# Batch 1's X units one loop step sooner, and a reordered opening, in a one-core Fourier mixer with an ELU MLP

## The chip, the cores and the metric

The kernel runs on one core of a Trainium2 chip. The core has a matrix engine (TensorE, PE in the profile, with PEld for its weight loads), a vector engine (VectorE, DVE), an activation engine (ScalarE, ACT), a general engine (GpSimd, POOL) and a queue engine (SyncE, SP) that issues DMAs. POOL issues DMAs too, on a queue of its own. Each engine works through its own instructions in program order; semaphores join them. The metric is the device time of one execution in microseconds (us).

## What is computed

The input x is 8 batches of 3008 tokens by 256 channels, in f32. For every batch a real Fourier transform runs along the tokens, a complex 256 x 256 product with a bias follows, each part is shrunk towards zero by 0.01, and the inverse transform goes back to tokens. The result passes an MLP with 2048 hidden columns and an ELU.

```python
X = np.fft.rfft(x, axis=1)
Yr = Xr @ w_r - Xi @ w_i + b_r
Yi = Xr @ w_i + Xi @ w_r + b_i
Yr = np.sign(Yr) * np.maximum(np.abs(Yr) - lam, 0.0)
y = np.fft.irfft(Y, n=x.shape[1], axis=1)
h = y.reshape(B * S, D) @ w_in
g = np.where(h > 0.0, h, np.exp(np.minimum(h, 0.0)) - 1.0)
out = g @ w_out
```

## The kernel before

**The transform as matmuls.** 3008 = 47 x 64, and the Fourier transform is split into two stages over these factors, as is its inverse. One batch passes these units:

- A (`unit_A`, lines 155 to 216; six per batch): the first stage, on a quarter of an x tile of 1 MB. Its result goes to the tile Z, in the opening by DMA straight from the copied block (`place`, L197), later through DRAM (DA, L216, and `load_Z`, L222).
- X (`unit_X`, L224; eight per batch): the second stage, Z times M2 (L237), copied into XT.
- M (`unit_M`, in the opening `first_M` and `last_M`; six pairs): the complex product with wcat, bias and shrinkage, giving Y. `turn_Y` (L428) turns Y through four DMAs on SP (L423).
- B (`unit_B`, in the opening `split_B`; six per batch): the first inverse stage. Its result goes to DRAM (DB) by a DMA on SP and comes back regrouped as Bs (`load_Bs`, L468).
- Y (`unit_Y`, `split_Y`, in the opening `first_Y`; eight per batch): the second inverse stage, Bs times M4, copied into yT.

**The loop.** Tokens are then taken in blocks of 512, and hidden columns in 8 pairs of 128. One step of the loop (line 1296) is one block and one pair: `front` computes two h tiles (L1098) and their exponential Et on ACT (L1110); `elu` clamps Et on POOL (L1149) or DVE (L1151); in the next step `finish_elu` forms gT on DVE (L1139); two steps later `back` multiplies by w_out (L1170) and stores a finished block from SP (L1191). A batch is 47 steps. While the loop works on batch b, the units of batch b+1, and the A units of batch b+2, are woven into its steps by `plan(b)` (L1200): list f0 of a step is issued ahead of `front`, list f1 behind it. For batch 0 the first step with an X unit of batch 1 is `FILL` (L1060); up to then the steps hold batch 1's A units (steps 0 to 5, with their DMAs to DRAM, `load_Z` in step 5) and the last Y units of batch 0 (`split_Y`, steps 7 to 9), which use a PSUM pool psG that is closed at step FILL. From FILL on, the list `mid` (L1206) is worked off one unit per step. `load_Bs` of batch 1 is issued in the step of B5 and in later steps.

**The opening.** All that is ahead of the loop is written out by hand (lines 612 to 1048), under a manual schedule, so the order of the program text is the order of each engine's queue. In turn:

1. `idle_pe(3)` (L620): filler matmuls on ones, while constants are built and x of batch 0 arrives by POOL's DMAs (`first_x`). An f32 matmul of the filler shows as two instructions.
2. The matrices M1d and M1c of the A units: cleared on ACT (L689), filled on DVE (L754, L761) from the sines r1 (L745, ACT). Z is cleared on ACT (L683).
3. Tables for X (M2) from DVE (`points`, `wraps`, `sizes`, `signs`, L805 to L835) and ACT (`sines`, L838), with a correction of its row 0 on DVE (`slot0`, L850); beside them on DVE the start of M3's tables (L863 to L869).
4. The six A units of batch 0 (L183). Units in `FOUR` sum four x rows per output with M1d (16 matmuls, one placing DMA), the others two with M1c (8 matmuls, two placing DMAs). Units run in two PSUM slots (pre2, two banks each), which ACT empties in order (L150); unit 5 runs in two single banks.
5. A second filler, `idle_pe(4)`, then the eight X units; the weights w_r and w_i come by SP and are cast to wcat on POOL, behind a gate (L911) and among `load_x` of batch 1.
6. The M pairs in the order 3, 4, 5, 0, 1, 2, with B units 3, 4, 5 between. Y is finished in halves: the last step of a pair that went over ACT is held and issued on DVE by `let_go` (L351). Pieces of w_in (`load_w_in` on SP, four) are scaled and cast to w_in_s on DVE or POOL (`scale_w_in`, L950). w_out comes in two halves by POOL (`load_w_out`, L945), each behind a `gate`, a small POOL copy that waits for a given tile (L958).
7. The seam: for B units 0 to 2, the part of Bs that the first Y units need is not sent through DRAM but turned on PE (`turn_B` L536, `turn_back` L559); the rest of it comes by `load_Bs(0, 0, 48)` (L474). Then `first_Y` (L577) and the remaining B units 0 to 2 (`split_B`, L492), whose copies and stores are issued by `store`.

Of the kernel before, what the change touches and what calls it, by code (L numbers as in the profile page):

```python
# [29 lines left out]
def kernel(  # L30
# [122 lines left out]
    FOUR = (0, 1, 2, 4, 5)  # L153

    def unit_A(b, u, alone=False, on_dve=False, apart=False):
# [324 lines left out]
    def split_B(v, ps, on_dve=(False, True), by_half=False):  # L480
# [24 lines left out]
        def store():  # L505
            for s in range(2):
                evac(Bv[:, s], ps[s][:].rearrange("p (q d) -> p q d", d=D), on_dve[s])
# [4 lines left out]
        return (lambda: half(1), store) if by_half else store  # L512
# [4 lines left out]
    def one_bank():  # L517
        return chain.tile([P, 512], F32, name="one", tag="one")
# [35 lines left out]
    def turn_back(dt):  # L554

        for h in range(2):
            ps = one_bank()
# [10 lines left out]
    def first_Y(dt):  # L568
# [4 lines left out]
        for h in range(2):  # L573
            ps = one_bank()
# [41 lines left out]
    def idle_pe(n):  # L616

        ones = busy[:].bitcast(F32)
        for _ in range(n):
            nc.tensor.matmul(  # L620
                ips[-1][:].rearrange("p (a b) -> p a b", a=2), lhsT=ones[:, 0:P],
                rhs=ones.unsqueeze(1).to_broadcast([P, 2, 256]), start=True, stop=True,
# [3 lines left out]
    idle_pe(3)  # L626
# [4 lines left out]
    with tc.tile_pool(name="stagep", bufs=1) as stagep:  # L631
# [61 lines left out]
        clear(M1d[:].rearrange("p q w -> p (q w)"))  # L693

# [51 lines left out]
        clear(M1c[:].rearrange("p q w -> p (q w)"))  # L746
        for h in range(2):
            clear_Z(h)
        c1 = mix(dve, qcol, -2.0, pcol, ALU.mult, ALU.add)
        c0 = col(dve, c1, -1.0, ALU.mult, 1.0, ALU.add)  # L750
        for h, c in enumerate((c0, c1)):
            for q in range(2):
                o = 3 * NS + 16 * h + 8 * q
                dve.tensor_scalar(  # L754
                    M1d[:, :, o : o + 8],
                    r1[:, NS * q : NS * q + NS].rearrange("p (b a) -> p a b", a=4),
                    c[:], None, ALU.mult,
                )
        r1v = r1[:].rearrange("p (q b a) -> p q a b", q=2, a=2)
        for h, c in enumerate((c0, c1)):  # L760
            dve.tensor_scalar(  # L761
                M1c[:, :, N2 + NS * h : N2 + NS * h + NS].rearrange("p a (q b) -> p q a b", q=2),
                r1v, c[:], None, ALU.mult,
            )
# [91 lines left out]
        def fA(u):  # L856
            unit_A(0, u, alone=True, apart=u == 5)
# [5 lines left out]
        dve.tensor_scalar(m3i[:], m3i[:], 63, None, ALU.bitwise_and)  # L863
        k3 = row("k3", [P, NV])
        dve.scalar_tensor_tensor(k3[:], m3i[:], float(N1), k1t[:], ALU.mult, ALU.add)
        dve.tensor_scalar(sg3[:], k3[:], S // 2 + 0.5, -0.5, ALU.is_gt, ALU.add)
        full = [P, NV, N2]
        k3b = k3[:].unsqueeze(2).to_broadcast(full)
        dve.scalar_tensor_tensor(  # L869
            v3[:], n2row.unsqueeze(1).to_broadcast(full), 1.0 / S, k3b, ALU.mult, ALU.mult  # L870
# [502 lines left out]
```

## Time and profile before

| what | value |
|---|---|
| median of the runs | 876.56 us (3 runs, 874.92 to 877.61) |
| the profiled execution | 874.79 us |
| its span in the trace | 873.0 us |
| PE busy | 862.9 us, 99% of the span |
| ACT, DVE, POOL busy | 713.9, 666.2, 587.1 us |
| first X unit of batch 0 on PE | 21.38 us |
| first `front` matmul | 45.71 us |
| first X unit of batch 1 on PE | 68.42 us |

Times in the profile count from the start of the span. A row of the timeline gives start, length, engine, line, operation, what is written from what, shape and count, and in brackets how long the engine was idle before and what ended that. A row of the waits gives engine and line that waited, for whom, total, number and longest. A row of the chain of waits gives start, length and what the end of the execution hung on at that time. SPq and POOLq are DMA issues. A busy PE need not be PE at its peak, since matmul ends are modelled.

### The profile page before, as it was taken

The page shows a single profiled execution, that of the slowest core. Times are in us where ns is not written, and L with a number is a line of the kernel's source. Part 1 is how long each engine was busy: PE and PEld are TensorE (multiplying, and loading weights), DVE is VectorE, ACT ScalarE, POOL GpSimd, SP SyncE. Part 2 cuts the span into 40 slices and gives each one's busy share as a digit, 9 for nine tenths or more (in the row PEclk, how much of TensorE's full clock was granted, in tenths as well). Part 3 has the DMA queues.
Part 4 walks back from the last instruction along what each step waited for, and adds up shares of the span by engine and source line. Part 5 has one row for each costly group of instructions (what it writes and reads, how often), then busy time and mean ns, then how long its engine had stood idle before and what let it go on. Part 6 is the DMA issues. An engine that isn't in the chain of part 4 may idle for free.

```text
span 873.0 us, 18541 instructions
## 1 busy us (share of the span) xinstructions
PE 862.9 (99%) x6768; PEld 675.8 (77%) x6768; DVE 666.2 (76%) x1110; ACT 713.9 (82%) x1251; POOL 587.1 (67%) x859
## 2 busy tenths in 40 slices
PE   9999999999999999999999999999999999999997
PEld 6567677887788877887779787788777878787776
DVE  8888778687776876768866787777777677788775
ACT  7778888888978889798887988879887888876664
POOL 7761640898757986588856888459874697734664
PEclk9999999999999999999999999999999999999999
DMA  8997346542474225743356442653337313250111
GB/s 242 297 279 200 112 113 191 166 143 76 122 242 130 89 73 147 217 147 101 94 169 182 133 110 73 203 160 119 100 89 214 97 38 86 75 144 25 39 36 49
DMA packets 115596, 116.11 MB, mean 133 GB/s; under 512 B 11552, under 2 KB 106016, under 8 KB 112144
## 3 DMA queue, kind: packets, MB, share of 16 engines
q1 hardware_dynamic: 109248, 87.40, 35.5%
q0 software_dynamic: 5968, 27.26, 9.9%
q8 instruction: 53, 0.87, 0.4%
q14 instruction: 39, 0.32, 0.1%
q10 hardware_dynamic: 288, 0.26, 0.1%
HBM read 53.28 MB, written 48.23 MB: 116 GB/s over the span
## 4 chain that ended last, share of the span: by engine, by line
PE 92%; POOL 2%; DMA 2%; DVE 1%; ACT 1%; issue 0%; SPq 0%; DVEq 0%; POOLq 0%
PE ps_o L1170 38%; PE hps L1098 34%; PE mps L329 5%; PE xps L237 3%; PE mps L1098 2%; PE yps L604 2%; PE bps L443 2%; PE aps L191 2%; PE mps L287 1%; PE ips L620 1%; DMA Bs<-DB 1%; PE aps L183 1%; POOL Y L345 1%; DMA DB<-Bz 1%; POOL yb L341 0%
## 5 line engine op out<-in xcount | busy, mean ns | idle before, releaser
L1139 DVE SCALAR_TENSOR_TENSOR gT<-Et,hps 128x512 fp32r<-128x512 f32 x630 | 402.9, 683 | 136.9 <-POOL Et L1149 127.0
L1170 PE MATMUL ps_o<-w_out_r,gT 128*128 128x256 f32 x3008 | 477.3, 301 | 0.0
L1170 PEld LDWEIGHTS ps_o<-w_out_r,gT 128*128 128x128 f32 x3008 | 404.4, 189 | 48.1 <-DVE osb L1182 0.2
L1149 POOL TENSOR_SCALAR Et<-Et 128x512 f32<-128x512 f32 x482 | 288.0, 617 | 209.3 <-ACT Et L1110 207.8
L1098 PE MATMUL hps<-yT,w_in_s 128*128 128x512 bf16 (+7 forms) x1620 | 366.1, 353 | 0.2
L1110 ACT ACTIVATE Et<-hps 128x512 f32<-128x512 f32 x514 | 282.5, 609 | 41.3 <-PE hps L1098 37.5
L1098 PEld LDWEIGHTS <-w_in_s 128*128 128x128 bf16 x1728 | 144.2, 98 | 103.9 <-issue 12.4
L1108 ACT ACTIVATE Et<-hps 128x512 f32<-128x512 f32 x192 | 104.6, 597 | 41.9 <-PE hps L1098 41.5
L1113 ACT ACTIVATE Et<-Et 128x512 f32<-128x512 f32 x192 | 110.4, 631 | 0.0
L345 POOL TENSOR_TENSOR Y<-yb,clip 128x512 bf16<-128x512 f32 x72 | 92.7, 1288 | 6.0
L341 POOL TENSOR_TENSOR yb<-yb,bias_bc 128x256 f32<-128x256 f32 x72 | 53.2, 739 | 11.4 <-DVE yb L336 11.4
L150 ACT CAST XT<-xps 128x768 bf16<-128x768 f32 x57 | 45.9, 805 | 13.7 <-PE xps L237 13.6
L150 ACT CAST yT<-yps 128x752 bf16<-128x752 f32 x56 | 44.1, 788 | 14.5 <-PE yps L604 14.5
L336 DVE TENSOR_TENSOR yb<-mps,yb 128x512 f32<-128x512 f32 x72 | 49.8, 692 | 7.6 <-PE hps L1098 0.5
L1141 DVE SCALAR_TENSOR_TENSOR gT<-hps,Et 128x512 fp32r<-128x512 f32 x78 | 50.2, 686 | 3.3
L150 ACT CAST A<-aps 128x1024 bf16<-128x1024 f32 x41 | 41.7, 1018 | 9.6 <-PE aps L191 4.9
L344 POOL TENSOR_SCALAR clip<-yb 128x512 f32<-128x512 f32 x72 | 44.3, 615 | 6.3
L150 ACT CAST Bz<-bps 128x1024 bf16<-128x1024 f32 x41 | 41.6, 1015 | 5.2 <-PE bps L443 4.9
L335 DVE TENSOR_TENSOR yb<-mps,bias_bc 128x256 f32<-128x256 f32 x72 | 30.5, 424 | 17.4 <-PE mps L329 15.6
L329 PE MATMUL mps<-wcat_s,XT 128*128 128x256 bf16 x288 | 43.2, 273 | 0.0
L1182 DVE COPY osb<-ps_o 128x512 f32<-128x512 f32 x46 | 31.7, 690 | 5.4 <-PE ps_o L1170 3.4
L255 POOL TENSOR_TENSOR XS<-XT 128x512 bf16<-128x512 bf16 x30 | 34.1, 1162 | 2.4 <-ACT XT L150 1.4
(208 smaller groups left out, 666.5 us busy)
## 6 DMA issues: line engine op xcount, KB each, us to landing
xt<-in_x_dram POOLq DMA_DIRECT2D x21, 1024.0 KB, 5.4
out_dram<-osb SPq DMA_DIRECT2D x158, 128.0 KB
Bs<-DB SPq DMA_DIRECT2D x30, 384.0 KB
Yx<-Y SPq DMA_DIRECT2D x168, 64.0 KB
DA<-A SPq DMA_DIRECT2D x19, 512.0 KB
DB<-Bz SPq DMA_DIRECT2D x19, 512.0 KB
Z<-DA SPq DMA_DIRECT2D x21, 384.0 KB
xt<-in_x_dram POOLq DMA_DIRECT2D x6, 512.0 KB, 5.8
```

The source lines that it names most:

```text
L150: nc.scalar.copy(dst, src)
L329: nc.tensor.matmul(out_, lhsT=lhs[:, dt] if lhs is not None else sum_of(dt, ch)[:, oc : oc + P], rhs=w[:, dt, :], start=(dt == 0), stop=(d ...
L341: nc.gpsimd.tensor_tensor(yb[:, D : 2 * D], yb[:, D : 2 * D], bias_bc[:, D : 2 * D], ALU.add)
L345: nc.gpsimd.tensor_tensor(Y_of[b, q][:, i, :], yb[:], clip[:], ALU.subtract)
L1098: nc.tensor.matmul(hps[s][:, c0:c1], lhsT=w_in_s[:, dt, ft * P : ft * P + P], rhs=yT_of[b][:, dt, t0 : t0 + c1 - c0], start=(dt == 0), sto ...
L1108: nc.scalar.activation(Et[:, s], hps[s], AF.Relu, scale=-1.0)
L1110: nc.scalar.activation(Et[:, s], hps[s], AF.Exp)
L1113: nc.scalar.activation(Et[:, s], Et[:, s], AF.Exp, scale=-1.0)
L1139: nc.vector.scalar_tensor_tensor(o, e, -1.0, h, ALU.add, ALU.max)
L1141: nc.vector.scalar_tensor_tensor(o, h, 0.0, e, ALU.max, ALU.add)
L1149: nc.gpsimd.tensor_scalar(e, e, 1.0, 0.0, ALU.min, ALU.max)
L1170: nc.tensor.matmul(po[q][:, i_ % 2, :], lhsT=gT[:, s, i_ * P : i_ * P + P], rhs=w_out_r[:, ft, :], start=(ft == 0 and i_ % 2 == 0), stop=( ...
```

## The change

It has two groups of edits.

*Loop.* `FILL` falls from 10 to 9, so that the list `mid` starts one step sooner and the `split_Y` units of batch 0 go to steps 6 to 8. In `mid`, B5 changes places with A0 and so stays in step 35; A3 goes ahead of the first two Y units, which stay in steps 39 and 40. The scaling of the second half of w_in piece 1 leaves step 1.

*Opening.* Unit A2 works with two x rows per output instead of four, in the two begin banks, each half copied and placed by itself. M1d and M1c are filled on ACT instead of DVE, with M1c cleared ahead of r1 and Z cleared behind the fills. M1 is filled on POOL instead of ACT. Parts of the tables change places: `signs(1)` and the second `sines(1, 1)` sooner, the m3i to v3 group later. Both fillers are half a matmul shorter. `load_w_in` 1 to 3 and the scalings of pieces 0 and 1 are issued sooner. `let_go` is issued once more ahead of `load_Bs`. Both halves of w_out are loaded without gates behind M4, with `load_x(1, 2)` between them, and so behind `load_Bs` in the program. At the seam, `split_B(1)` goes between the halves of `turn_B(2)`, the copies of `split_B(0)` are split (the ACT half ahead of `turn_back`, the DVE half and the store behind it), and the pool chain of four banks becomes chain and chain2 of two.

```diff
-    FOUR = (0, 1, 2, 4, 5)
+    FOUR = (0, 1, 4, 5)
...
-            pair = two_banks(pre1, "mps1") if alone else two_banks(psG, "gps")
+            if alone:
+                pair = two_banks(begin, "begin") if u == 2 else two_banks(pre1, "mps1")
+            else:
+                pair = two_banks(psG, "gps")
...
-            if alone:
+                if alone and u not in FOUR:
+                    place(2 * j, 2 * j + 2)
+            if alone and u in FOUR:
                 place(0, 4)
...
-    idle_pe(3)
+    idle_pe(2)
+    idle_pe(1, 1)
...
         clear(M1d[:].rearrange("p q w -> p (q w)"))
+        clear(M1c[:].rearrange("p q w -> p (q w)"))
...
         nc.scalar.activation(r1[:], v1[:], AF.Sin, bias=0.0, scale=TURN / 4.0)
-        clear(M1c[:].rearrange("p q w -> p (q w)"))
-        for h in range(2):
-            clear_Z(h)
...
-                dve.tensor_scalar(
+                nc.scalar.activation(
                     M1d[:, :, o : o + 8],
                     r1[:, NS * q : NS * q + NS].rearrange("p (b a) -> p a b", a=4),
-                    c[:], None, ALU.mult,
+                    AF.Copy, scale=c[:],
                 )
...
+            for q in range(2):
+                nc.scalar.activation(
...
+        for h in range(2):
+            clear_Z(h)
...
-            unit_A(0, u, alone=True, apart=u == 5)
+            unit_A(0, u, alone=True, apart=u in (2, 5))
...
         sizes(1)
+        signs(1)
+        dve.tensor_scalar(m3i[:], m3i[:], 63, None, ALU.bitwise_and)
...
         slot0()
+        for h, c in enumerate((c0, c1)):
+            pool.tensor_scalar(M1[:, N2 * h : N2 * h + N2], r1[:], c[:], None, ALU.mult)
         sines(1, 0)
+        sines(1, 1)
...
-        load_x(1, 2)
         for q, i in ((3, 0), (3, 1)):
             begin_M(q, i)
-        idle_pe(4)
+        idle_pe(3)
+        idle_pe(1, 1)
...
     load_w_in(0)
+    load_w_in(1)
...
     fB(3)
-    load_w_in(1)
+    load_w_in(2)
     first_M(5, 1, True)
+    for c in range(2):
+        scale_w_in(0, True, c)
     first_M(0, 0, False)
     fB(4)
-    scale_w_in(0, True, 0)
+    for c in range(2):
+        scale_w_in(1, True, c)
     first_M(0, 1, True)
     fB(5)
-    gate(Bz_of[0, 2][:, 7, 0:1])
-    load_w_out(0)
+    let_go()
     load_Bs(0, 0, 16 * NT)
-    load_w_in(2)
+    load_w_in(3)
     first_M(1, 0, False)
-    scale_w_in(0, True, 1)
-    scale_w_in(1, True, 0)
...
-    load_w_in(3)
     M4v = M4[:].rearrange("p (a h) -> p a h", h=2)
...
+    load_w_out(0)
+    load_x(1, 2)
+    load_w_out(1)
     first.close()
...
     turn_B(2, (0,), two_banks(chain, "one"), True)
-    turn_B(2, (1,), two_banks(chain, "one"), True)
-    store_0()
-    rest_1, store_1 = split_B(1, two_banks(lateB, "lateB"), (True, True), True)
+    rest_1, store_1, _ = split_B(1, two_banks(lateB, "lateB"), (True, True), True)
+    turn_B(2, (1,), two_banks(chain2, "one"), True)
+    copy_0(0)
     turn_back(0)
     turn_back(1)
+    store_0((1,))
     rest_1()
-    gate(Y_of[0, 2][:, 1, 0:1])
-    load_w_out(1)
...
-    FILL = 10
+    FILL = 9
...
-            ("B", 2), ("M", 5, 0), ("M", 5, 1), ("B", 3), ("B", 4), ("B", 5), ("A", 0),
-            ("A", 1), ("A", 2), ("n", 0), ("n", 1), ("A", 3), ("A", 4), ("A", 5),
+            ("B", 2), ("M", 5, 0), ("M", 5, 1), ("B", 3), ("B", 4), ("A", 0), ("B", 5),
+            ("A", 1), ("A", 2), ("A", 3), ("n", 0), ("n", 1), ("A", 4), ("A", 5),
...
-                (7, f0, 2), (7, f1, 3), (8, f0, 4), (8, f1, 5), (9, f0, 6), (9, f1, 7)
+                (6, f0, 2), (6, f1, 3), (7, f0, 4), (7, f1, 5), (8, f0, 6), (8, f1, 7)
...
-            f1[1].insert(0, (scale_w_in, (1, True, 1)))
```

More of the change, by code (lines that the diff above doesn't have):

```diff
@@ L510, in store, with one_bank @@
             )
-        return (lambda: half(1), store) if by_half else store
+        return (lambda: half(1), store, copy_out) if by_half else store
     NT = 3
     turned = []
-    def one_bank():
-        return chain.tile([P, 512], F32, name="one", tag="one")
+    def one_bank(dt):
+        return (chain2 if dt else chain).tile([P, 512], F32, name="one", tag="one")
     def turn_B(v, ts=(0, 1), ps=None, on_dve=False):
```

54 lines of the change are left out of this document (26 added, 28 removed).

## The prediction

> **What bounds the kernel now.** I read the page first (busy times), then the TensorE (PE) waits, then the timeline of the first 75 us and of 113 to 145 us, the chain of waits there, and the DMA issues with their landings.
>
> ```profile
> span 873.0 us, 18541 instructions
> PE 862.9 (99%) x6768; PEld 675.8 (77%) x6768; DVE 666.2 (76%) x1110; ACT 713.9 (82%) x1251; POOL 587.1 (67%) x859
> ```
>
> PE is busy for 862.9 of 873.0 us, so a change pays only if it removes PE work, PE filler, or one of PE's waits. The waits of PE over the whole span are short; these are the five that matter here (us in total, times, longest):
>
> ```profile
> PE yps L604 <- DMA Bs<-DB: 0.7, 1, 0.7
> PE one L577 <- DMA Bs<-DB: 0.5, 1, 0.5
> PE lateB L536 <- DVE Y L351: 0.5, 1, 0.5
> PE bps L443 <- DMA Yx<-Y: 0.4, 1, 0.4
> PE lateA L492 <- DVE Y L351: 0.3, 1, 0.3
> ```
>
> They sum to 2.4 us. Three of them (one, lateB, lateA) stand at the seam between the opening and the loop, two (bps, yps) at the border from batch 0 to batch 1. What else can be won is filler and A work ahead of the first X unit, because all that follows shifts with it.
>
> **Opening, up to X.** The timeline (start, length):
>
> ```profile
> 1.45 4.62 PE L620 MATMUL ips<-busy 128*128 128x512 f32 x6 [1.45 <-DVE busy L613]
> 4.13 0.26 ACT L745 ACTIVATE r<-v 128x64 f32<-128x64 f32 x1 [1.07 <-DVE v L744]
> 4.22 1.95 POOL L121 DMA_DIRECT2D xt<-in_x_dram  x3
> 4.46 0.81 DVE L754 TENSOR_SCALAR M1d<-r,c 128x32 fp32r<-128x32 f32 x4
> 4.71 3.70 ACT L683 ACTIVATE Z<-busy 128x2048 f32<-128x2048 bf16 x2
> 5.53 6.29 PE L183 MATMUL aps<-xt,M1d 128*128 128x256 f32 x48
> 8.32 0.98 ACT L150 CAST A<-aps 128x1024 bf16<-128x1024 f32 x1
> 12.93 2.16 PE L183 MATMUL aps<-xt,M1d 128*128 128x256 f32 x16 [0.15 <-ACT A L150]
> 17.02 0.59 ACT L150 CAST A<-mps 128x512 bf16<-128x512 f32 x1 [0.36 <-PE mps L183]
> 17.66 3.70 PE L620 MATMUL ips<-busy 128*128 128x512 f32 x8
> 19.11 0.38 DVE L850 TENSOR_SCALAR M<-M,c 128x24 bf16<-128x24 bf16 x2 [0.34 <-ACT M L838]
> 19.40 1.14 DVE L835 SCALAR_TENSOR_TENSOR a<-a,c,sw 128x384 f32<-128x384 f32 x2
> 19.71 0.58 ACT L904 ACTIVATE M<-r,c 128x64 fp32r<-128x64 f32 x2
> 21.38 0.84 PE L237 MATMUL xps<-M,Z 128*128 128x96 bf16 x16
> ```
>
> The reader sees a chain: A units on PE, the last A copy on ACT until 17.61, filler from 17.66 to 21.36, X at 21.38. The last copy and the filler set the start of X.
>
> *Unit A2 twofold.* It falls from 16 to 8 matmuls. At 6.29/48 = 0.13 us each that is 1.05 us of PE work gone. It also moves to the begin banks, so that A4 no longer waits for A2's copy (the 0.15 in its row). Begin's banks are next used by the two bias matmuls after A5, long after A2's copy. A2 gets one placing DMA more on SP, an issue of some 0.57 us (two take 1.14 in the row of 131.60 below). Its two halves are copied by ACT in about the time of one whole copy and more than 3 us ahead of A5's copy, so SP is free again when A5's own DMA is due, and nothing behind it is late.
>
> *Fills move from DVE to ACT.* DVE loses the M1d fill (0.81) and the M1c fill (two instructions, so less than another 0.81). ACT gains eight copies of 128x32, four for each tile. No row shows one; the nearest is L904, 0.29 each for twice the width, the lower end is nothing. I take 0.23, so M1d is full at 4.39 + 4 x 0.23 = 5.3, just ahead of the A0 start at 5.53, and M1c at 6.2. Clearing Z (3.70) follows: 9.9 instead of 8.41. So A0's copy starts at 9.9 instead of 8.32, which nobody needed earlier, except that A3 takes A0's banks (10.9) and A4 takes A1's (11.9). With 2.0 us for each of A4 and A5 (2.16 with the last matmul's tail), A5 ends near 15.8 and its second copy (0.59) near 16.4, against 17.61: **1.2 us** sooner; 0.9 if a fill costs 0.29 and 1.5 if 0.2. The x tiles do not stop this:
>
> ```profile
> xt<-in_x_dram POOLq DMA_DIRECT2D x2, 512.0 KB, 7.4
> ```
>
> This is the row of the last two issues; the last is issued by 6.17 and so lands by 13.6, before A5 starts at 13.8.
>
> *Filler.* The second filler falls from 8 to 7 instructions' worth: 3.70/8 = **0.46 us**. The first loses as much at its slower pace, 4.62/6 = 0.77, but A0 is held there by M1d, so I count nothing. X could then start 1.67 sooner. Two things can hold it. Z's last DMA is issued at A5's copy; it landed at the latest 21.36 - 17.61 = 3.75 after it, so Z alone allows 1.2 at worst. M2's row 0 (L850) ended at 19.49; DVE loses 0.8 to 1.6 ahead of it and gets signs(1) (1.14) put ahead, so it ends between 19.0 and 19.8, just before the new start of about 19.8. The moved group m3i to v3 only changes place ahead of it. On ACT the last sine goes ahead of bias_bc, and M1 (0.58) leaves ACT for POOL; behind it on POOL stand the gate, load_x(1,0) and the wcat copies, which wait for that last sine anyway, and the sine comes sooner by A5's 1.2 and by the M1 and bias_bc that no longer stand ahead of it. I take 1.6 for the start, less 0.1 for DVE's w3, which then meets the second X copy: **-1.5 us** (0.9 to 1.9). The list of waits has none between X and lateB, so the M stage is a row of PE work and shifts along. load_w_in(1) and (2) are issued sooner on SP, but behind w_r and w_i, on which the M stage waits.
>
> **Seam to the loop.** Old times:
>
> ```profile
> 33.97 0.42 DVE L950 TENSOR_SCALAR w_in_s<-w_in_f 128x512 bf16<-128x512 f32 x1
> 36.09 0.69 DVE L297 TENSOR_TENSOR yb<-mps,bias_bc 128x512 f32<-128x512 f32 x1 [1.70 <-issue]
> 36.35 0.98 POOL L945 DMA_DIRECT2D w_out_r<-in_moe_w_out_dram  x1
> 37.29 2.39 DVE L950 TENSOR_SCALAR w_in_s<-w_in_f 128x512 bf16<-128x512 f32 x2
> 39.39 1.01 POOL L1022 TENSOR_SCALAR M<-r,w 96x47 bf16<-96x47 f32 x2
> 39.60 0.68 DVE L351 SCALAR_TENSOR_TENSOR Y<-begin,clip 128x512 bf16<-128x512 f32 x1
> 42.40 0.68 DVE L148 CAST A<-lateA 128x512 bf16<-128x512 f32 x1
> 43.00 1.27 DVE L148 CAST Bs<-one 48x512 bf16<-48x512 f32 x2
> 45.71 1.04 PE L1098 MATMUL hps<-yT,w_in_s 128*128 128x512 bf16 x4
> 48.80 1.10 PE L1170 MATMUL ps_o<-w_out_r,gT 128*128 128x256 f32 x8
> ```
>
> The two scalings of 2.39 us hold the Y at 39.60, for which PE waits 0.5 and then 0.3. They go ahead of 36.09, where DVE idles 1.70; the row of 33.97 shows one at 0.42, so that two (0.8) fit there, and the other pair goes before 33.97, at worst 0.8 against a Y that PE needs for B4. So both waits should vanish. The added let_go stands in the same idle stretch and only brings a Y forward. Behind them DVE does the A copy (42.40), the Bs copies (43.00), and the yT copies, after which hps starts at 45.71. The Bs copies lose the two waits (0.8) and the A copy ahead of them (43.00 - 42.40 = 0.6), 1.4 in all if PE's turning is as early; then the A copy (0.6) comes ahead of the yT copies instead, so that 1.4 - 0.6 = 0.8 remains, with 1.1 if part of the A copy falls into an idle moment. ACT's own A copy still stands ahead of its half of Bs, and the hand-overs from PE to copy and back keep their lengths, so 0.3 is the low end. I take **-0.7 us** on top of the shift. The pool split in chain and chain2 keeps four banks in the same turn, so it costs nothing. Bs's own load must come in time:
>
> ```profile
> 36.17 3.16 DMA DB<-Bz
> 39.40 4.92 DMA Bs<-DB
> ```
>
> Bs landed at 44.32 and is now wanted 0.7 sooner, against the shift. With w_out's first half (issued 36.35) out of both, 3.16 + 4.92 should shrink by more than that. What is late next is w_out:
>
> ```profile
> w_out_r<-in_moe_w_out_dram POOLq DMA_DIRECT2D x1, 1024.0 KB, 7.1
> ```
>
> It now goes out behind M4 (39.39 and 1.01, perhaps 0.6 sooner, so 39.8), needs some 7.1 and is used at 48.80 - 0.7 = 48.1: 1.2 us to spare, so no cost. load_w_in(3) waits on SP behind Bs's load as before, load_x(1,2) and w_out(1) on POOL behind w_out(0); the first of them is needed at step 4, four steps later.
>
> **Loop.**
>
> ```profile
> 49.07 1.09 ACT L1110 ACTIVATE Et<-hps 128x512 f32<-128x512 f32 x2 [0.67 <-DVE gT L1139]
> 70.57 0.51 PE L237 MATMUL xps<-M,Z 128*128 128x96 bf16 x8
> 71.24 0.32 POOL L958 CAST gate<-Z 128x1 f32<-128x1 bf16 x1 [2.86 <-DMA Z<-DA]
> 131.60 1.14 SPq L461 DMA_DIRECT2D DB<-Bz  x2
> 136.42 3.03 DMA Bs<-DB
> ```
>
> *Scaling gone from step 1.* Et of step 1 waits 0.67 for gT of step 0, since two w_in pieces still hold the other buffers of that tag. With both halves of piece 1 scaled early, a buffer is free. ACT gains 0.67; PE, which is stretched a little there, I give **-0.3** (0 to 0.7).
>
> *X one step sooner.* split_Y moves along, so steps only trade work; a POOL clamp at step 9 goes to DVE, which has room. But X2 now comes at X1's old place plus one X unit, 70.57 + 0.51 = 71.1, and needs the second part of Z, which the gate saw at 71.24: **+0.2** (0 to 0.6).
>
> *Border.* M5 comes a step sooner, A0 takes its place ahead of B5, which stays in step 35, so Yx is there and 0.4 goes. B4's store went out together with B5's (131.60, two issues); now it goes a step earlier, the first Bs piece need not wait for it, and the last piece (3.03) travels with less beside it. The 0.7 at yps should shrink to 0.1 or so: **-0.9** (0.3 to 1.1). A1's and A3's stores on SP stand as before behind the Bs loads. Batch 2's last A units and its Z come a step sooner, where PE has no wait to lose.
>
> **Sum**: -1.5 - 0.7 - 0.3 + 0.2 - 0.9 = **-3.2 us**. The profiled execution took 874.79 us (span 873.0), so 871.6; it lies 1.8 under the median of the runs, 876.56, from which I forecast **873.4**.
>
> **Rivals.**
> (1) *Z does not shift.* x(1,2) and w_out(1) are now loaded later and run beside A, DA and Z of batch 1. If Z lands where it did (71.24) while PE comes for it at 71.1 - 2.5 = 68.6, PE waits 2.6 instead of 0.2, and 875.8 comes out: within 0.3%. For it speaks the 2.86 us wait at the gate, against it that Z is issued after A5, which shifts.
> (2) *w_out shares its queue* and ends on the other side: three 1 MB loads (w_out(0), x(1,2), w_out(1)) now leave POOL together. If they are served in turns, the first takes two to three times 7.1; at twice, it lands at 39.8 + 14.2 = 54.0 against 48.1, PE waits 5.9 at the first back, and 879.3 comes out. It decides from 8.3 us of landing on, and turns the sign from 11.5. Against it: the x tiles, six loads of one queue, fed the A units one after the other without PE waiting for them. [...]
> (3) *The clock comes late.* The first filler passes take 0.77, the later ones 0.46: the clock rises in the first filler. Were A0's 16 matmuls run at half speed, that costs 2.1 us of PE, of which about 1.5 reach X: 874.9. Against it: A0's start stays at 5.53, so PE is as busy until then as before, but for some tenths. [...]
> (4) *The moves do nothing*: X held by Z's DMA, seam by yT copies, yps by the store: 876.5.
>
> **Chances.** Forecast with its bounds 0.69 (871.0 to 875.5), rivals (1) 0.11, (2) 0.09, (3) 0.05, (4) 0.06. About 0.3%, or 2.6 us, is what a measurement of this kernel can tell from no change; faster by that means under 873.9. The forecast gives 0.57 of that; the rest of it (0.12) with (1), (3) and (4) makes 0.34 for the same, and (2) 0.09 for slower. The range of 871.0 to 876.2 takes in the bounds and (1).
>
> **What would show it.** X's first matmul near 19.9; no waits at lateB, lateA and one; hps first near 43.5; ps_o first without a wait for w_out; Et of step 1 without a wait; xps waiting under 0.6 for Z; no bps wait and yps under 0.3. Wrong it is if A0's copy starts past 10.5, if PE waits for w_out, or if X2 waits for Z by more than 1 us.

## The result and the profile after

The changed kernel takes 877.63 us (median of 20 runs, 876.05 to 881.77) where the kernel before takes 875.68 (20 runs beside it): a ratio of 1.0025, 95% interval 1.0014 to 1.0036. Measured a second time, in another set of runs, the ratio is 1.0021 (1.0006 to 1.0036). So the change costs about 2 us, where 3.2 us of gain were forecast. The profiled execution took 876.69 us, with a span of 874.9 against 873.0.

The page of the changed kernel, span and busy times:

```profile
span 874.9 us, 18527 instructions
PE 861.8 (98%) x6760; PEld 675.0 (77%) x6760; DVE 666.4 (76%) x1104; ACT 714.7 (82%) x1258; POOL 587.7 (67%) x859
```

PE is busy for 1.1 us less (862.9 before), about half of the 2.3 us that A2's eight matmuls (1.05) and the two fillers (0.77 and 0.46) were priced at, and yet the span is 1.9 us longer. So the time went into waits of PE. Here is its list of waits (for whom, total, times, longest):

```profile
PE gps L598 <- DMA Bs<-DB: 2.6, 1, 2.6
PE xps L242 <- DMA yb<-in_w_i_dram: 1.3, 1, 1.3
PE ps_o L1184 <- DVE A L148: 0.8, 1, 0.8
PE bps L448 <- DMA Yx<-Y: 0.2, 1, 0.2
```

Three new waits, 4.7 us together, stand where four of the five old ones (yps, one, lateB, lateA; 2.0 us together) are gone. The second and the third name a releaser that is not the true one, and that shows only when one looks up what the instruction waits for. X's first weight load waits for all eight placing transfers of Z and for VectorE, but not for w_i; the first ps_o waits for w_out, not for an A copy of VectorE. The timeline of the changed kernel at these places:

```profile
4.42 1.06 ACT L761 ACTIVATE M1d<-r,c 128x32 fp32r<-128x32 f32 x4
5.39 0.95 ACT L769 ACTIVATE M1c<-r,c 128x32 fp32r<-128x32 f32 x4
6.24 3.70 ACT L692 ACTIVATE Z<-busy 128x2048 f32<-128x2048 bf16 x2
9.85 1.89 ACT L150 CAST A<-aps 128x1024 bf16<-128x1024 f32 x2
16.76 0.58 ACT L150 CAST A<-mps 128x512 bf16<-128x512 f32 x1 [0.36 <-PE mps L186]
22.02 0.84 PE L242 MATMUL xps<-M,Z 128*128 128x96 bf16 x16 [1.34 <-DMA yb<-in_w_i_dram]
44.54 1.21 PE L1112 MATMUL hps<-yT,w_in_s 128*128 128x512 bf16 x4
48.75 1.18 PE L1184 MATMUL ps_o<-w_out_r,gT 128*128 128x256 f32 x8 [0.79 <-DVE A L148]
61.02 0.51 PE L598 MATMUL gps<-M,Bs 96*128 96x94 bf16 x8 [2.59 <-DMA Bs<-DB]
```

The last A copy ends at 17.34 instead of 17.61, X starts at 22.02 instead of 21.38: the distance grew from 3.77 to 4.68 us. From X to the first hps it is 22.52 us instead of 24.33. Then ps_o waits for w_out and gps for Bs.

If one pairs the hps matmuls of the two traces one by one, the lead of the changed kernel can be read as a running account: 1.17 us ahead at the first, level after the first ps_o, 0.16 ahead just before the wait for Bs, **2.9 to 3.3 behind** after it, some 4 behind while work that stood later before is done (X and M units a step sooner), back to 2.5 at the border of the batches and to 2.0 just after it, where it stays to the end. In this execution all is decided in the first 61 us.

Other executions lose in a second way, which this one does not show. In the second set of runs the mean granted TensorE clock of an execution is 0.992 to 0.998 in all 12 of the changed kernel (0.9958 on average), while 16 of the 27 of the kernel before have 0.999 or more (0.9985 on average); of the first 20 of the changed kernel 3 have that. The trace of e16, the changed kernel again, shows where: its clock is at 0.50 from 23.2 to 26.6 us and from 64.2 to 67.6, right behind the ends of waits of 2.8 us for Z and 4.5 us for Bs, and PE works at a lower pace there. The second X unit of batch 0 in the trace above, and in e16:

```profile
23.40 1.00 PE L242 MATMUL xps<-M,Z 128*128 128x96 bf16 x16 [0.21 <-ACT XT L150]
```

```profile
24.18 1.48 PE L242 MATMUL xps<-M,Z 128*128 128x96 bf16 x16
```

The two means differ by 0.0027, which is 2.4 us of 877: an estimate, and an upper one, since the mean also counts time in which PE waits. The medians of that set differ by 2.2. So a long wait can cost more than its own length; how the loss divides between the waits and the lower clock behind them, no run separates.

### The profile page after: what moved, and what is told of

It reads as the page before. It is cut to its first block, busy times and chain, and to the rows that moved or that the text cites. A ratio compares the mean times of both kernels' runs of the same rounds, so it can differ in the third digit from the quotient of the medians.

```text
span 874.9 us, 18527 instructions
## 1 busy us (share of the span) xinstructions
PE 861.8 (98%) x6760; PEld 675.0 (77%) x6760; DVE 666.4 (76%) x1104; ACT 714.7 (82%) x1258; POOL 587.7 (67%) x859
## 4 chain that ended last, share of the span: by engine, by line
PE 90%; DMA 3%; POOL 2%; ACT 2%; DVE 1%; issue 1%; SPq 0%; DVEq 0%; POOLq 0%
PE ps_o L1184 38%; PE hps L1112 33%; PE mps L334 5%; PE xps L242 2%; PE mps L1112 2%; PE yps L612 2%; PE bps L448 2%; PE aps L194 2%; PE mps L292 2%; DMA DB<-A 1%; POOL Y L350 1%; DMA Yx<-Y 1%; POOL yb L346 0%; DMA Bs<-DB 0%; POOL clip L349 0%
## 5 line engine op out<-in xcount | busy, mean ns | idle before, releaser
L340 DVE TENSOR_TENSOR yb<-mps,bias_bc 128x256 f32<-128x256 f32 x72 | 30.5, 424 | 17.5 <-PE mps L334 15.7
```

## The experiments

Four theories were set up in turn. **Train theory (T):** three loads of 1 MB each (w_out(0), x(1,2), w_out(1)) now leave POOL together at 40 to 42 us and hold up SP's stores of DB, so that Bs for the moved `split_Y` comes late. **Steps theory (S):** the moved `split_Y` outrun Bs by themselves. **Filler theory (H):** in the kernel before Z landed only just under the filler, so that less filler brings nothing. **w_in theory (L):** w_in(1), now loaded behind w_in(0), delays Z. L fell, and the **bunching theory** took its place: the placing transfers of Z start later and queue. Each line of the table is a comparison with the kernel before in the same set of runs.

| run | median us | ratio to before | 95% interval |
|---|---|---|---|
| e1_x12_back | 873.30 | 0.9978 | 0.9967 to 0.9988 |
| e2_steps_back | 875.10 | 0.9996 | 0.9985 to 1.0007 |
| e3_steps_only | 875.19 | 0.9995 | 0.9984 to 1.0006 |
| e4_wout_old | 876.18 | 0.9998 | 0.9982 to 1.0014 |
| e5_before_short_filler | 876.04 | 0.9993 | 0.9976 to 1.0010 |
| e7_win1_pool | 878.12 | 1.0018 | 1.0004 to 1.0032 |
| e8_x12_win_pool | 876.84 | 0.9992 | 0.9976 to 1.0007 |
| e9_x12_wout0_early | 877.33 | 1.0004 | 0.9986 to 1.0022 |
| e6_a2_back | 878.37 | 1.0020 | 1.0006 to 1.0034 |
| e10_fills_dve | 877.01 | 1.0007 | 0.9993 to 1.0021 |
| e11_wout1_gate | 874.10 | 0.9973 | 0.9960 to 0.9987 |
| e13_x12_a2_fills | 874.88 | 0.9985 | 0.9974 to 0.9997 |
| e14_x12_fills | 874.20 | 0.9974 | 0.9961 to 0.9988 |
| e15_x12_fills_wout1_late | 873.63 | 0.9966 | 0.9951 to 0.9982 |
| e16_change_again | 878.78 | 1.0021 | 1.0006 to 1.0036 |

### The late Bs: train or steps

**e1**: the changed kernel with one line moved back.

```diff
         pool.tensor_scalar(idm[:], prow, pcol[:], None, ALU.is_equal)
+        load_x(1, 2)
...
     load_w_out(0)
-    load_x(1, 2)
     load_w_out(1)
```

> The changed kernel with load_x(1, 2) back in its old place, right behind load_x(1, 1); both halves of w_out stay behind M4. Theory T (the train): three 1 MB loads leave POOL together at 40.3 to 42.8 us, and beside them the store of B unit 1 (DB<-A, issued 46.7) takes 10.1 us to land, so that Bs for split_Y is late. Without x in the train w_out(1) should land near 51.5, DB<-A by 53, Bs by 57.5, and the gps wait of 2.6 should fall to 0.3 or less: 2.4 us under the changed kernel, about 875.2. Rival S (the steps): split_Y one step sooner outruns Bs by itself, whatever is loaded beside it: the wait stays above 2 and the time near 877.6.

873.30, below both kernels, and 1.9 us below what T expected. The wait for Bs is gone, that of the first ps_o stays. The waits of PE in this run:

```profile
PE xps L242 <- DMA w_in_f<-in_moe_w_in_dram: 3.1, 1, 3.1
PE ps_o L1184 <- DMA w_out_r<-in_moe_w_out_dram: 0.9, 1, 0.9
```

No gps is in it. The profiled execution is one of the longer of its runs (875.57), with X as late as 23.15; that late X also gave Bs more time, so the profile alone would not decide. The median does, with the next two runs. It came down by 4.3 us where T had 2.4; the mean granted clock rose too, to 0.9986 from the 0.9966 of the first 20 executions of the change (a difference of 0.0020, or 1.8 us of 875, an estimate as above).

**e2** has the changed opening with the loop of before (`FILL` 10, `mid` and `split_Y` as they were), **e3** the kernel before with only the loop changed.

```diff
-    FILL = 9
+    FILL = 10
...
-                (6, f0, 2), (6, f1, 3), (7, f0, 4), (7, f1, 5), (8, f0, 6), (8, f1, 7)
+                (7, f0, 2), (7, f1, 3), (8, f0, 4), (8, f1, 5), (9, f0, 6), (9, f1, 7)
```

> The changed kernel with the loop's order undone: FILL 10, mid and the split_Y steps as before; the opening stays changed. Both theories: split_Y comes a step (some 2.3 us) later, so the gps wait falls from 2.6 to about 0.3; at the border bps and yps wait again for about 1.0 together where now only 0.2 is seen. T and S: about 877.6 - 2.3 + 0.8 = 876.1. It prices the opening alone: if the train costs PE anything beside the gps wait, that stays here (the first ps_o waits 0.8).

> The kernel before with the loop's order alone changed: FILL 9, the new mid, split_Y in steps 6 to 8; the opening and its loads as before. T: Bs lands as before, by about 58, and is wanted at 58.5; a gps wait of 0.4 at most, X2 waits for Z by 0.3 at most, the border waits go (1.0 to 0.2): 0.2 to 0.8 us under the kernel before. S: a gps wait of 1.5 or more, and 0.7 us or more over the kernel before.

875.10 and 875.19: neither is slower than before. e3 has no wait for Bs in `split_Y` at all (the Bs piece landed at 59.3 and was read at 62.06), so the earlier steps alone do not outrun Bs, and S falls. e2 still waits 0.6 us for it a step later. Only both together make the 2.6.

**e4**: w_out behind its old gates and x(1,2) in its old place.

```diff
     let_go()
+    gate(Bz_of[0, 2][:, 7, 0:1])
+    load_w_out(0)
     load_Bs(0, 0, 16 * NT)
...
-    load_w_out(0)
-    load_x(1, 2)
-    load_w_out(1)
...
     rest_1()
+    gate(Y_of[0, 2][:, 1, 0:1])
+    load_w_out(1)
```

> The changed kernel with the three POOL loads where they were: load_x(1, 2) behind load_x(1, 1), w_out(0) gated behind B unit 5, w_out(1) gated behind Y of pair 2. T: no gps wait, no ps_o wait (0.8 now); the wait for Bs at the seam (0.5 before) may come back: 877.6 - 2.6 - 0.8 + 0.5 = 874.7. S: the gps wait stays, about 877.3.

876.18 and no gain, where T had 874.7. In the trace gps and ps_o no longer wait, as T says, and instead the first Y unit waits for the Bs of the seam, which now travels beside w_out(0):

```profile
PE one L585 <- DVE A L148: 1.9, 1, 1.9
PE xps L242 <- DVE A L921: 1.2, 1, 1.2
```

So moving w_out(0) behind the load of Bs did what it should at the seam, and is part of the 1.1 us by which the seam beat its forecast. But this wait does not explain the median: the profiled execution has it, and took only 873.02. Its granted clock is 0.999; nine of the twelve executions have 0.997 or less, and why they do no trace shows.

That the train's length is the cause shows in the last store of DB ahead of Bs (B unit 1), over all traces. Issue times are rows of the timeline; the landings are the trace's records of the transfers' semaphores.

| kernel | 1 MB loads on POOL in the 8 us ahead | store issued | lands after |
|---|---|---|---|
| e4, e3 | 1 | 47.38, 50.33 | 3.8, 4.3 us |
| e9, before | 1 | 49.82, 47.76 | 4.9, 5.1 |
| e15, e5 | 1 | 45.11, 48.95 | 5.4, 5.8 |
| e1 | 2 | 48.76 | 7.6 |
| e11, e13, e14, e8 | 2 | 46.22, 46.73, 45.33, 47.26 | 8.1, 8.1, 8.3, 8.3 |
| changed kernel, e10 | 3 | 46.69, 45.13 | 10.1, 10.1 |
| e7, e2, e16, e6 | 3 | 45.97, 47.23, 48.08, 47.66 | 10.5, 10.6, 10.9, 11.0 |

One load ahead makes 4 to 6, two make 8, three make 10 to 11. In the changed kernel it ends the chain of waits (start, length):

```profile
46.69 10.12 DMA DB<-A
56.87 4.10 DMA Bs<-DB
```

and SP stands at the load of Bs for 7.2 of these 10 us: it issues nothing from 49.67 to 56.87. The store is 256 KB in rows of 512 bytes, and each load has four times its data, in packets of 1 KB (w_out) or 8 KB (x). In the trace of the changed kernel the stores did move beside the loads, but the last one only ended with them: the three stores of DB landed at 53.3, 55.8 and 56.8, the loads at 48.6, 51.2 and 56.2.

### X: where Z's landing comes from

**e5**: the kernel before with a second filler of half its length.

```diff
-        idle_pe(4)
+        idle_pe(2)
```

> The kernel before with idle_pe(2) in place of idle_pe(4) as second filler, 1.85 us less, so that X starts when Z has landed and no later. From the end of A5's copy to X it was 3.77 us before; in the changed opening it is 4.7, 5.4, 6.4 and 4.5 us in four profiles. Rival H (hidden): Z landed just before 21.4 also in the kernel before, the filler only covered it; X stays within 0.3 us of 3.77 after the copy, the time at 875.9. Theories L (loads issued behind Z slow it) and P (the later clearing of Z bunches the placing DMAs): Z landed well before; X comes 2.5 to 3.2 us after the copy, the time 0.5 to 1.2 lower.

H holds. In this run the last A copy ends at 18.71 (the clock rose late, see the last section), the filler is over before X, and X starts 3.71 us after the copy, with a wait; in the kernel before it was 3.77 without one:

```profile
22.42 0.84 PE L237 MATMUL xps<-M,Z 128*128 128x96 bf16 x16 [1.68 <-DVE A L907]
```

Z's landing was the bound all along, hidden under a filler that ended at the same moment. The landings say the same: in every one of the 17 traces X starts 0.3 to 0.5 us behind the last part of Z's transfers (before: 21.07 and 21.38; changed kernel: 21.60 and 22.02).

**e7** moves w_in(1) from SP to POOL, behind x(1,1); **e8** does the same with w_in(0) and w_in(1), on top of e1, with x(1,1) and x(1,2) behind them; **e9** puts w_out(0) right behind x(1,2), on top of e1.

```diff
...
     load_w_in(0)
-    load_w_in(1)
+    load_w_in(1, nc.gpsimd)
```

> The changed kernel with load_w_in(1) alone moved from SP, where it stands right behind w_in(0) and so 1.7 us behind Z's last placing DMA, to POOL behind load_x(1, 1). L: Z lands some 3.8 us after A5's copy, X starts near 20.5, about 1 us under the changed kernel, 876.6. P: X stays 4.5 us or more behind the copy, 877.6.

> The kernel of e1 with w_in(0) and w_in(1) both on POOL, behind load_x(1, 0) and ahead of load_x(1, 1) and (1, 2): behind Z's last DMA only w_r and w_i (256 KB each) follow on SP. L: X right behind the filler, near 20; against e1 (873.3) 1.5 us less, 871.8. P: X 4.5 us or more behind the copy, 873.3.

> The kernel of e1 with the first half of w_out right behind load_x(1, 2) on POOL, ahead of the X units, in place of behind M4. T: the first back no longer waits for w_out (0.9 in e1), and DMA was idle around 34 and 41 us there: 872.4. If the 1 MB slows the stores of B units 3 to 5 instead, Bs waits at the seam (one L585) by 0.5 or more and nothing is won: 873.3 or more.

In e7 and e8 X still starts 4.67 and 5.23 us after the copy, so w_in behind Z is not the cause: L falls. Neither gains time: e7 came to 878.12, and e8 to 876.84, 3.5 us over e1, from which it was to differ by -1.5 or nothing. Its trace has a wait of 1.8 us for Z of batch 1 and one of 0.9 for Bs that e1 has not; what makes them is open. e9 does away with the ps_o wait, as it should, but its X came at 23.64 and its median is 877.33, where 872.4 or 873.3 were expected. What it loses against e1 (1.0004 to 0.9978) is not explained by a wait for w_out; the records show one of the sixteen parts of Z's last transfer at 23.23, where fourteen were there by 21.01. Behind this wait of 3.7 us the granted clock is at 0.50 from 22.4 to 29.2, and over its executions it is 0.9961 on average, against 0.9986 in e1. Why Z came so late there is open.

**e6** undoes A2's halves, **e10** brings the fills of M1d and M1c back to VectorE, so that ScalarE clears Z 2.0 us and copies A0 1.5 us sooner. (The expectations of e6, e11, e13 and e15 count batches from 1: what they call batch 1 is batch 0 here.)

```diff
-    FOUR = (0, 1, 4, 5)
+    FOUR = (0, 1, 2, 4, 5)
...
-            unit_A(0, u, alone=True, apart=u in (2, 5))
+            unit_A(0, u, alone=True, apart=u == 5)
```

```diff
-                nc.scalar.activation(
+                dve.tensor_scalar(
                     M1d[:, :, o : o + 8],
...
-                    AF.Copy, scale=c[:],
+                    c[:], None, ALU.mult,
```

> The changed kernel with one part undone: the third A unit of batch 1 is again copied whole and placed in Z with one transfer of 256 KB instead of two of 128 KB. Open is why Z lands 4.2 us after the issue of A5's placing transfer with the change and 3.4 us before it. Bunching theory: with the change the placing transfers stand closer together (first issue 10.85 instead of 9.32, last 17.37 instead of 17.63), the four half transfers take 0.7 to 1.0 us each on the queue where a whole one takes 1.0 to 1.1, and so the last one queues. Then one whole transfer saves about 0.7 us of the queue: A5's transfer lands 3.4 to 3.7 us after its issue, X starts 21.2 to 21.5, and the time falls by 0.4 to 0.7 against the changed kernel (877.0), since the late Bs at the border of the batches (2.6 us) stays. Neighbour theory: what delays Z are the loads behind it (w_r, w_i, x of batch 2); then nothing changes, 4.2 us and X at about 22, 877.6.

> The changed kernel with the eight fills of M1d and M1c on VectorE again (four and two instructions), so that ScalarE clears Z at about 4.7 instead of 6.24 and copies A0 at about 8.3 instead of 9.85. Bunching theory: the first placing transfers leave 1.5 us sooner, the queue has emptied when A5's comes, which lands about 3.5 us after its issue instead of 4.2; A2's halves stay. X starts 21.2 to 21.5 in place of 22.0, 877.0. Neighbour theory: no change of the distance from A5's copy to X, about 4.7. Third view, that VectorE's fills hold the points and signs up by 1.3 us and with them the sines: then M2 and not Z would be last, and X would start at about 22 with the wait put down to ScalarE.

In e6 the A units are held up by each other: the last copy is at 18.23, X at 22.99 (the first row is ScalarE, the second PE).

```profile
18.23 0.59 ACT L150 CAST A<-mps 128x512 bf16<-128x512 f32 x1 [0.36 <-PE mps L186]
22.99 0.84 PE L242 MATMUL xps<-M,Z 128*128 128x96 bf16 x16 [0.85 <-ACT bias_bc L919]
```

The expectation put X at 21.2 to 21.5; it overlooked that a whole A2 puts 8 matmuls (1.05 us) back and, as A0's copy is late, a wait of 0.37 us ahead of A2; the clock rose later too in this run. The transfer itself came sooner after its issue (15 of 16 parts 3.3 us, all 3.9), but this run cannot price that. e10 can. The same two rows there:

```profile
15.96 0.59 ACT L150 CAST A<-mps 128x512 bf16<-128x512 f32 x1 [0.36 <-PE mps L186]
20.46 0.84 PE L242 MATMUL xps<-M,Z 128*128 128x96 bf16 x16 [0.58 <-DVE A L917]
```

X starts at 20.46 (expected was 21.2 to 21.5), 1.56 sooner than in the trace of the change, 0.6 and 0.8 sooner than in e4 and e7, whose last copies end within 0.1 us of this one, and 0.92 sooner than before. The placing transfers, in issue and landing (all 16 parts):

| kernel | first issued | A5's issued | A5's landed | after |
|---|---|---|---|---|
| before | 9.32 | 17.63 | 21.07 | 3.4 us |
| e3, e5 (old opening) | 10.27, 10.21 | 18.78, 18.73 | 22.16, 22.12 | 3.4, 3.4 |
| changed kernel | 10.85 | 17.37 | 21.60 | 4.2 |
| e4, e7 (fills as changed) | 10.86, 10.87 | 16.62, 16.65 | 20.69, 20.89 | 4.1, 4.2 |
| e1, e2, e8 (fills as changed) | 10.85, 10.85, 10.85 | 16.79, 16.52, 16.54 | 22.74, 21.44, 21.34 | 5.9, 4.9, 4.8 |
| e9, e11, e16 (fills as changed) | 10.86, 10.86, 10.85 | 16.61, 16.53, 16.58 | 23.23, 21.14, 22.30 | 6.6, 4.6, 5.7 |
| e10, e14, e15 (fills on DVE) | 9.41, 9.44, 8.89 | 16.57, 16.60, 16.39 | 20.05, 20.16, 20.01 | 3.5 to 3.6 |
| e6 (A2 whole), e13 (A2 whole, fills on DVE) | 10.85, 8.90 | 18.84, 17.52 | 22.69, 21.56 | 3.9, 4.0 |

With the fills ahead of Z's clearing eight transfers go out in 5.7 to 6.5 us, where before seven had 8.3, and the last lands at the end of a queue; with the fills on VectorE they have 7.2 to 7.5, and it lands after 3.5 us, nearly as before. That the order of the fills is the cause is shown by e10, e14 and e15 against nine traces with the fills as changed; that a queue of transfers is the link is read from these times, and no run varied it alone. That the four halves add to it is argued only: in e4's records 128 KB takes the queue 0.7 to 1.0 us, 256 KB takes 0.9 to 1.1, but e13, with A2 whole, lands no sooner than e10 does with halves. In the trace of the changed kernel a half, of 8 rows in its pattern, counts 8 landings (behind one count some 1.1 us after the issue), and a whole one, of 16, counts 16.

e10's median is only 877.01. In its trace what X won runs into the Bs wait, now 3.6 us; but that execution took 875.02, the shortest of its twelve, and eleven of them have a granted clock of 0.998 or less, so the wait is not the whole of it.

### Both causes undone

> The changed kernel with x(1,2) loaded where it was loaded before and w_out(1) behind its old gate on Y; w_out(0) alone stays ungated. Train theory: it is the length of what POOL queues ahead of SP's stores of DB that delays them. With w_out(0) alone ahead (1 MB) the store that took 10.1 us with three loads and 7.6 us with two should take about 4 to 6, Bs for batch 1's last B units is there in time, and w_out(0) lands in less than the 8.3 to 8.5 us that it took in company, about 6, so that the first ps_o no longer waits 0.8. 872.5 to 873.3, the same as or up to 0.8 better than with w_out(1) ungated (873.3). Rival, that two loads are no worse than one: 873.3 and both waits as there; and if w_out(1) behind the gate now lands later than the first step that reads it, a wait on it shows in step 1 and it comes out above 874.

**e11** (e1 with w_out(1) behind its old gate) tells little apart: the gate opened at once, w_out(1) left 1.1 us after w_out(0) instead of 1.0, and store (8.1), ps_o wait (1.2) and ratio (0.9973) are close to those of e1. Its expectation, a store of 4 to 6 us and 873.3 at most, was missed.

> Three parts undone together: x(1,2) loaded where it was, the third A unit whole, the fills of M1d and M1c on VectorE. What is left of the change is the opening's order on VectorE and POOL, w_out ungated, the seam and the earlier units of batch 1. If the bunching theory and the train theory both hold, their gains add: X starts at 20.9 to 21.4 (A5's transfer 3.4 us after its issue), no Bs wait; 872.3 to 872.9, below x(1,2) alone (873.3) by 0.4 to 1.0. If only the train theory holds: 873.3.

**e13** (e1, e6 and e10 together) came to 0.9985, where less than e1's 0.9978 was expected: A2 whole puts the last A copy back to 17.5, and X starts at 21.86, where e14, the same but for A2's halves, has 20.66. That speaks for the halves, though the intervals of e13 and e14 overlap.

> Two parts undone together: x(1,2) loaded where it was, and the fills of M1d and M1c on VectorE, so that the placing transfers leave 1.5 us sooner; the third A unit stays twofold. If the queue of placing transfers and the length of the train of loads are the two causes of the miss, the two gains add: X starts at about 20.5 as with the fills alone (22.0 with the change, 21.4 before), and no or little wait for Bs at the border. Against x(1,2) alone (873.3 where before was 875.9) 0.8 to 1.5 less: a ratio of 0.9960 to 0.9972, 872.0 to 873.0. Rival: what X gains is given back at the first ps_o and at Bs, which wait for loads that start and end with the seam, and the time stays at that of x(1,2) alone, ratio 0.9978.

> As the run with x(1,2) and the fills undone, and w_out(1) behind a gate on the last copy of batch 1's B unit 1, so that it leaves at about 46 us, after SP's last store of DB, and one load of 1 MB is ahead of the stores in place of two. Train theory: that store takes 4 to 5.5 us (3.8 and 4.9 with 1 MB ahead, 7.6 to 8.1 with 2 MB, 10.1 to 11.0 with 3 MB), w_out(0) alone lands in 5 to 6.5 us, so the first ps_o waits at most 0.3 instead of 0.8 to 1.2, and Bs is in time. w_out(1) lands at about 54 to 55, before the step that reads it first (about 57). 0.8 to 1.2 less than without the gate: ratio 0.9950 to 0.9962. Rivals: the store takes as long as before whatever is ahead of it (then 0.9965 as without the gate), or w_out(1) comes after its reader, a wait on it of 1 to 3 us in the fifth step (0.9975 to 1.0).

> The changed kernel itself, beside the two others on the same chip, so that their distance to it is measured and not put together from two jobs. Both theories: 1.0025 again, 1.001 to 1.0036; the store of DB issued at about 46.7 takes about 10 us, Bs is waited for by 2 to 3.6 us, and A5's placing transfer lands 4.1 to 4.3 us after its issue.

**e14** is e1 and e10 together, **e15** adds a gate that sends w_out(1) off behind SP's last store of DB, **e16** is the changed kernel again beside them.

```diff
     load_w_out(0)
-    load_w_out(1)
...
     store_1()
+    gate(Bz_of[0, 0][:, 7, 0:1])
+    load_w_out(1)
     second.close()
```

In this set before took 876.59, the change 878.78, e14 874.20 and e15 873.63. PE's waits in e14 and then in e15:

```profile
PE gps L598 <- DMA Bs<-DB: 1.1, 1, 1.1
PE ps_o L1181 <- DVE A L148: 0.8, 1, 0.8
PE xps L242 <- DVE A L917: 0.8, 1, 0.8
```

```profile
PE ps_o L1182 <- DVE gT L1151: 1.2, 1, 1.2
PE xps L242 <- DVE A L917: 0.7, 1, 0.7
```

e14's ratio (0.9974) is within the spread of e1's (0.9978): what X wins with the fills is largely given back at gps, as its rival said. In e15 the store takes 5.4 us, Bs is in time, and 0.9966 is reached, 5.2 us under the change itself and the best median ratio of all; its interval overlaps with those of e1, e11 and e14. Both ratios lie outside what was expected (0.9960 to 0.9972 and 0.9950 to 0.9962). e16 came out as expected in its ratio, but its Bs wait (4.5) and A5's landing (5.7 behind the issue) were longer. In e15 w_out(0), now alone, did not land sooner, and the first ps_o waited 1.2 instead of 0.3. The DMA issues of the changed kernel and of e15 (size, us to landing):

```profile
w_out_r<-in_moe_w_out_dram POOLq DMA_DIRECT2D x1, 1024.0 KB, 8.3
```

```profile
w_out_r<-in_moe_w_out_dram POOLq DMA_DIRECT2D x1, 1024.0 KB, 8.6
```

So it is not its followers on POOL that slow it. By the packet records its first packet starts 3.0 and 3.3 us after the issue in these two, and 2.0 and 1.8 in the kernel before and in e4, where it is issued ahead of the seam's Bs and of w_in(3) and not behind them. That these two delay it is only argued from the records; no run took them away.

## Why the prediction was wrong

**The sum.** The terms were -1.5, -0.7, -0.3, +0.2 and -0.9. Measured: X +0.64 in place of -1.5 (2.1 missed); the seam -1.8 in place of -0.7 (1.1 better); ps_o +0.8 and gps +2.6, for which the sum had nothing. The forecast of -3.2, less these, gives +1.2 against +1.9 measured on the spans; the rest is not settled.

**X: the step that failed is "which nobody needed earlier".** A's copies came as forecast: fills of 0.24 to 0.27 each (0.23 assumed), A0's copy at 9.85 (9.9), A5's copy 0.27 sooner in this profile, where x came 0.33 late, and about 1.0 sooner in e2, e4, e7 and e10 (1.2 forecast). But A0's copy was needed earlier, by the placing transfers behind it. The prediction counted SP's issues and found SP free, and took Z's landing after A5's copy as a constant of at most 3.75. It was the bound before (e5); from the end of A5's copy to X it was 3.77 and became 4.7 here, and up to 7.1 in other executions (e9); the filler that was cut had only hidden it. e10 shows that the order on ScalarE is the cause: with the fills on VectorE X comes at 20.46, -0.9 of the -1.5.

**Seam: right in kind, too small.** lateB, lateA and one no longer wait. e4, which loads w_out(0) ahead of the seam's Bs again, has 1.9 us of wait there; the prediction had given that move no gain.

**w_out: "needs some 7.1 and is used at 48.1: 1.2 us to spare".** It left at 40.29 instead of 39.8 and needed 8.3. Rival (2) named 8.3 as the point from which it decides, and the wait of 0.8 is what came. But its mechanism, that the three loads share POOL's queue in turns, is not what happened: they landed in order (48.6, 51.2, 56.2), and alone it is no quicker (e15).

**Steps: "split_Y moves along, so steps only trade work".** This is the costliest failed step, 2.6 us here and 4.5 in e16's profile. The prediction asked who needs the three loads, and when; it did not ask whose transfers they would run beside. Rival (1) did ask that, but for Z of batch 1 and not for DB and Bs, which are needed a step sooner by the same change. e1 takes one load out of the train, and the ratio goes from 1.0025 to 0.9978, some 4 us. The sum had also no term for what a long wait does to the clock behind it, which the result section shows in e16.

**Border and Et: right.** bps waits 0.2 (0.4 before), yps no longer; the account moves from 3.9 behind to 2.0 across the border, of which the X and M work done sooner is a part. Et of step 1 has no wait on VectorE left:

```profile
47.27 1.13 ACT L1124 ACTIVATE Et<-hps 128x512 f32<-128x512 f32 x2
73.85 0.50 PE L242 MATMUL xps<-M,Z 128*128 128x96 bf16 x8 [0.25 <-ACT Et L1124]
```

X2 of batch 1 waits 0.25 in the second row, as forecast (0.2), though Z was seen at the gate only at 73.87, 2.6 us later than the 71.24 from which the forecast worked. PE came about as much later, behind gps, so that the size agrees by luck.

## What to carry to other kernels

A transfer that waits for nothing is not free: here a store of 256 KB landed after 10.1 us beside three loads of 1 MB, and after 5.1 with one ahead of it. Before several large loads are put side by side, list the small transfers on the other queues that are in flight in the same ten microseconds, and who waits for them. A filler that ends when a transfer lands hides that transfer from the list of waits (X came 3.77 us after the copy under the filler of before, without a wait, and 3.71 in e5 with one of 1.68); before cutting it, shorten it alone and see whether the next instruction moves. And when an early copy is let slip because its reader has time, look at the DMA behind it too, since transfers pushed together landed later here than transfers spread out (4.1 to 6.6 us after the issue with the fills and A2 as changed, 3.5 to 3.6 with the fills back on VectorE). Read the granted clock of all executions, and not of the profiled one alone: a long wait of PE can be followed by some microseconds at a lower clock (in e16 3.4 us at 0.50, behind waits of 2.8 and of 4.5).

## What the runs showed of the hardware

**A store beside loads.** A 256 KB store from SP in rows of 512 bytes landed after 3.8 to 5.8 us with one load of 1 MB ahead of it on POOL, after 7.6 to 8.3 with two and 10.1 to 11.0 with three.

**One part late.** In some executions one of the sixteen parts of a transfer comes late by itself: in e16 fifteen parts of A5's transfer were there by 20.55 and the last at 22.30, and PE started X at 22.71; e1, e9 and e11 show the same for one or two parts (0.8 to 2.2 us behind the rest), before, e3, e5, e10, e14 and e15 do not. Where a single landing is the bound, the start varies by this much, and what sets it is open.

**The clock.** In the opening the pace of PE's f32 matmuls rises at one moment, for those of the A units from 0.21 us each to 0.12 and for the filler in the kernel before from 0.85 to 0.45, and this moment is not the same in every execution: by the record of the granted clock 4.7 us from the start in the changed kernel, 5.0 in the kernel before, 7.2 and 7.3 in e1 and e6, 7.6 and 7.5 in e3 and e5, whose programs are those of before up to there; over all 17 traces it lies between 4.3 (e11) and 7.6. The A0 row of e5, against 5.53 and 6.29 in the kernel before:

```profile
5.94 6.98 PE L183 MATMUL aps<-xt,M1d 128*128 128x256 f32 x48
```

This puts the whole opening up to 1.1 us later in one execution than in another; what sets the moment, no run shows. Rival (3) is therefore at work in some executions of all these kernels, and the cut filler is not needed for it: e3 and e5 run the uncut first filler.

**The clock behind a wait.** It can fall to 0.50 again, for 3.4 or 6.8 us, late in a wait of PE or within 2 us behind it: at the wait for Z in e1, e2, e8 and e16 (1.9 to 3.1 us of wait, 3.4 us of low clock) and in e9 (3.7 and 6.8), at the wait for Bs in e16 (4.5 and 3.4) and e6 (3.8 and 6.8), at a wait of 1.9 at the seam in e3 and of 1.2 at ps_o in e15 (3.4 each). It does not always: e10 waited 3.6 and e7 3.1 for Bs without it. From X to the first hps it was 22.5 to 22.6 us in the changed kernel, e6, e7, e10, e11, e14 and e15, 23.2 to 23.5 in e1, e2, e8 and e16, and 24.0 in e9.

**GpSimd.** A fill of 128x64 that ScalarE did in 0.29 us (two in 0.58, L904 before) took GpSimd 0.9 (two in 1.81 us, L911).
